# Fewer warm products, the first q in parts, a lent staging buffer and a new table of order

## The chip, the cores and the metric

The kernel runs on one core of a Trainium2 chip. The metric is device time of one launch in microseconds. Three runs of the kernel before gave 1077.51, 1078.24 and 1081.42 us; the median is 1078.24 us.

The core's engines run their own queues of instructions and wait for one another by semaphores. PE multiplies matrices (it also transposes, as a product with an identity), DVE and ACT work on rows of elements, POOL does the same more slowly, and SP issues DMAs. All data are float32.

## The reference

Attention in which only scores within `tau` of the row's largest count, then two feed-forward layers:

```python
scores = scale * q @ k.T                                  # q, k, v: 4 x 8 x 576 x 64
thresh = max(scores, axis=-1) - tau
scores = where(scores >= thresh, scores, -1e9)
attn = exp(scores - max(scores)); attn /= sum(attn) + 1e-9
x = (attn @ v) -> [2304, 512]                             # heads side by side
x = (s * relu(x @ w_in) ** 2 + b) @ w_out                 # 512 -> 2048 -> 512
h = x @ w2_in; y = (relu(h) + alpha * min(h, 0)) @ w2_out # 512 -> 2048 -> 512
```

The weights arrive as 64-bit words and are turned into float32 on the chip.

## The kernel before, in words

Three stages overlap. Attention handles 16 pairs of heads; a pair has nine score tiles of 128 rows by 576 columns. For each, PE makes the scores (line 1394), DVE takes the row maximum (1404), POOL a threshold from it (1406), ACT the exponential (1408), and DVE masks and sums (1410). The tile `e` that comes out is transposed on PE (`flip`, lines 917 to 921: all transposes of a group in the fast type in line 919, the last of a group in plain float32 in line 921, unless PE goes straight on to another group of transposes, when `plan.joined` puts that one in the fast type too), copied by ACT (1522) and multiplied by `v` (1534). The first four pairs, 36 score tiles, work in plain float32, with two buffers `sc` for the scores; the other twelve split each operand into a high and a low part and use three products.

The first feed-forward layer is cut into units of 256 hidden columns. Ten of its hidden tiles (`NA`) are prepared early, during attention: each half unit is loaded by SP into one of two staging buffers `stg` (1007, 1012), and joined to float32 in one of two buffers `n32` by DVE and ACT: line 1022 or 1024 (ACT or DVE, whichever the plan chooses), then 1028 and 1030 on DVE, the sign by 1060 on ACT and 1062 on POOL, the high part by 1066 on ACT, the low part by 1067 on POOL or DVE. The product tiles stand in `wa`. Blocks of tokens are multiplied in lines 1136 to 1138, three products for one.

The second layer, after attention, uses a scheme of seven products for eight (`seven`).

The order is not the code's. `Plan.add` records tasks, each with an engine (or several), a duration, buffers that it needs, and a rank. `Plan.run` lays them out: whenever an engine is free it takes the ready task of the lowest rank whose buffers are free. `MOVES` adds a number to the rank of task n. Buffers are slots with a count. The result is a fixed order per engine; every engine then works in that order on the chip and waits where data are late. SP waits likewise, in order, so one waiting load holds back all loads behind it.

Warm products (`warm`, line 1492) multiply the identity with itself into a spare bank: 12 at the start (`FILL`), 7 behind transposes of the first pair (`FILLS`), 3 behind each of the first two scores (`FILL1`) and 2 behind each of the other 34 of the first four pairs (`FILL2`), 93 in all. A warm product is two records in the trace.

For the first pair, SP loads k (1268) and q in one DMA each, and ACT issues the two tails (1284). PE transposes the four blocks of q; then DVE scales the copy for head 0 and ACT that for head 1 (1328, 1330).

## Time and profile before

| what | value |
|---|---|
| median of three runs | 1078.24 us |
| the profiled execution | 1078.0 us, of which 1076.0 us from the first instruction to the last |
| PE busy | 1056.9 us (98%) |
| DVE busy | 876.9 us (81%) |
| ACT busy | 695.0 us (65%) |
| POOL busy | 357.1 us (33%) |
| DMA engines, mean rate | 159 GB/s |

The busy time of an engine is the union of its instructions, so a stretch with overlapping products counts once. The shares are means over stages with different limits; the stage tables among the rows below cut them apart. The 2.0 us around the span are the launch.

### The profile page before, as it was taken

The page shows a single profiled execution, that of the slowest core. Times are in us where ns is not written, and L with a number is a line of the kernel's source. Part 1 is how long each engine was busy: PE and PEld are TensorE (multiplying, and loading weights), DVE is VectorE, ACT ScalarE, POOL GpSimd, SP SyncE. Part 2 cuts the span into 40 slices and gives each one's busy share as a digit, 9 for nine tenths or more (in the row PEclk, how much of TensorE's full clock was granted, in tenths as well). Part 3 has the DMA queues.
Part 4 walks back from the last instruction along what each step waited for, and adds up shares of the span by engine and source line. Part 5 has one row for each costly group of instructions (what it writes and reads, how often), then busy time and mean ns, then how long its engine had stood idle before and what let it go on. Part 6 is the DMA issues. An engine that isn't in the chain of part 4 may idle for free.

```text
span 1076.0 us, 21525 instructions
## 1 busy us (share of the span) xinstructions
PE 1056.9 (98%) x7210; PEld 1008.9 (94%) x7210; DVE 876.9 (81%) x1989; ACT 695.0 (65%) x1636; POOL 357.1 (33%) x494
## 2 busy tenths in 40 slices
PE   8899999999999999999999999999999999999998
PEld 7677899999989899989999999999999999999998
DVE  5989888888898888847967686588988999898882
ACT  5888878878887788744442355465756776565550
POOL 2666746744764466420000021120111344112110
PEclk9999999999999999999999999999999999999999
DMA  7754375566365644425476767249664664554531
GB/s 183 190 163 141 97 177 131 149 165 153 98 156 139 150 106 111 122 75 189 139 244 201 259 211 230 79 132 291 223 228 158 196 206 140 150 145 141 146 99 40
DMA packets 182127, 170.90 MB, mean 159 GB/s; under 512 B 56065, under 2 KB 160513, under 8 KB 182017
## 3 DMA queue, kind: packets, MB, share of 16 engines
q1 hardware_dynamic: 179248, 167.50, 54.5%
q10 hardware_dynamic: 2768, 2.03, 0.7%
q8 instruction: 56, 0.92, 0.4%
q14 instruction: 55, 0.44, 0.1%
HBM read 98.97 MB, written 49.28 MB: 138 GB/s over the span
## 4 chain that ended last, share of the span: by engine, by line
PE 86%; DVE 6%; ACT 3%; DMA 3%; issue 2%; SPq 0%; POOL 0%; DVEq 0%; ACTq 0%; POOLq 0%
PE bank L1136 14%; PE bank L1137 13%; PE bank L1138 13%; PE bank_b L1137 8%; PE bank_b L1138 8%; PE bank_b L1136 8%; PE sc L1394 7%; PE bank L1554 5%; PE bank L919 4%; PE bank L921 3%; PE bank L1492 1%; PE bank L1534 1%; DVE e L1410 1%; DVE wb L1114 1%; DMA stg<-in_moe_w_in_dram 1%
## 5 line engine op out<-in xcount | busy, mean ns | idle before, releaser
L1410 DVE SCALAR_TENSOR_TENSOR e<-sc,mx,e 128x576 f32<-128x576 f32 x144 | 116.2, 811 | 12.9 <-ACT e L1408 9.0
L1404 DVE TENSOR_REDUCE mx<-sc 128x1 f32<-128x576 f32 x144 | 107.6, 751 | 22.4 <-PE sc L1394 21.6
L1408 ACT ACTIVATE e<-sc,mx 128x576 f32<-128x576 f32 x144 | 106.6, 742 | 12.9 <-DVE mx L1404 12.4
L1136 PE MATMUL bank<-xt,wa 128*128 128x480 f32 (+3 forms) x235 | 87.0, 370 | 1.2 <-ACT rest L1676 0.8
L1406 POOL TENSOR_SCALAR mx<-mx,tau_s 128x1 f32<-128x1 f32 x144 | 51.2, 357 | 87.5 <-DVE mx L1404 80.3
L1137 PE MATMUL bank<-xt,wa 128*128 128x480 f32 (+3 forms) x235 | 79.1, 337 | 0.0
L1138 PE MATMUL bank<-xt,wa 128*128 128x480 f32 (+3 forms) x235 | 79.1, 336 | 0.0
L921 PE MATMUL bank<-eyes_r,e 128*128 128x128 f32 (+1 forms) x238 | 68.9, 291 | 0.5 <-DVE e L1410 0.5
L1554 PE MATMUL bank<-gl,vt 128*128 128x256 f32 (+1 forms) x192 | 63.6, 332 | 0.0
L1136 PE MATMUL bank<-gt,wa 128*128 128x384 f32 (+3 forms) x173 | 62.2, 360 | 0.6 <-ACT gw L1868 0.3
L1137 PE MATMUL bank<-gt,wa 128*128 128x384 f32 (+3 forms) x173 | 59.7, 345 | 0.0
L1138 PE MATMUL bank<-gt,wa 128*128 128x384 f32 (+3 forms) x173 | 59.7, 345 | 0.0
L1554 PE MATMUL bank<-gh,vt 128*128 128x256 f32 (+1 forms) x192 | 57.7, 302 | 0.0
L1592 DVE TENSOR_TENSOR gl<-bank,gh 128x256 fp32r<-128x256 f32 (+1 forms) x96 | 43.4, 452 | 10.9 <-ACT gh L1590 9.1
L1394 PE MATMUL sc<-k,q 128*128 128x288 f32 x232 | 49.0, 337 | 3.3 <-DMA q<-hq 1.5
L1101 POOL TENSOR_TENSOR sm<-stg 128x256 f32<-128x256 f32 x8 | 6.6, 835 | 135.3 <-DMA stg<-wfi 125.3
L1602 POOL TENSOR_TENSOR gr<-gf,gh 64x256 fp32r<-64x256 f32 (+1 forms) x48 | 38.9, 811 | 35.1 <-DVE gl L1600 28.3
L1136 PEld LDWEIGHTS bank<-xt,wa 128*128 128x128 f32 x235 | 45.1, 192 | 3.8 <-ACT rest L1676 1.2
L1590 ACT ACTIVATE gh<-bank 128x256 fp32r<-128x256 f32 (+1 forms) x96 | 39.4, 411 | 12.7 <-PE bank L921 5.5
L1138 PEld LDWEIGHTS bank<-xt,wa 128*128 128x128 f32 x235 | 44.1, 188 | 2.4
L1030 DVE SCALAR_TENSOR_TENSOR n<-stg,n 128x512 int32<-128x512 int32 x64 | 45.5, 710 | 0.8
L1137 PEld LDWEIGHTS bank<-xt,wa 128*128 128x128 f32 x235 | 44.5, 189 | 0.7
(686 smaller groups left out, 4190.5 us busy)
## 6 DMA issues: line engine op xcount, KB each, us to landing
stg<-in_moe_w_in_dram SPq DMA_DIRECT2D x32, 512.0 KB, 4.2
stg<-in_moe_w_out_dram SPq DMA_DIRECT2D x32, 512.0 KB, 4.0
gf<-gw SPq DMA_DIRECT2D x41, 192.0 KB, 3.2
q<-hq SPq DMA_DIRECT2D x24, 256.0 KB, 4.7
qo<-hq SPq DMA_DIRECT2D x24, 256.0 KB, 4.6
gw<-gf SPq DMA_DIRECT2D x47, 128.0 KB, 2.9
xt<-xs SPq DMA_DIRECT2D x14, 384.0 KB, 4.6
yf<-yb SPq DMA_DIRECT2D x24, 192.0 KB, 2.6
```

The source lines that it names most:

```text
L921: nc.tensor.transpose(to, part(x), one)
L1030: add("DVE", dve(DM), lambda: nc.vector.scalar_tensor_tensor(ni(), word(0), 29, ni(), op0=ALU.logical_shift_right, op1=ALU.bitwise_or), (n ...
L1136: nc.tensor.matmul(o, lhsT=wl, rhs=mh, start=first, stop=False, skip_group_check=on_top)
L1137: nc.tensor.matmul(o, lhsT=wh, rhs=ml, start=False, stop=False, skip_group_check=on_top)
L1138: nc.tensor.matmul(o, lhsT=wh, rhs=mh, start=False, stop=last, skip_group_check=on_top)
L1394: nc.tensor.matmul(sp.t[:, x, :HS], lhsT=o[0][:, c], rhs=o[1][:, x * HS:(x + 1) * HS], start=n == 0, stop=n == len(passes) - 1)
L1404: add("DVE", dve(S), lambda sp=sp, mx=mx: nc.vector.tensor_reduce(mx.t[:, 0:1], sp.t[:, :, :HS], op=ALU.max, axis=AX.XY, negate=True), (sp ...
L1406: t2 = add("POOL", 0.26, lambda mx=mx: nc.gpsimd.tensor_scalar(mx.t[:, 1:2], mx.t[:, 0:1], -1.0, tau_s, op0=ALU.mult, op1=ALU.subtract), ( ...
L1408: add("ACT", act(S, 1), lambda sp=sp, mx=mx, e=e: nc.scalar.activation(halves(e.t), sp.t[:, :, :HS], AF.Exp, bias=mx.t[:, 0:1]), (sp, mx), ...
L1410: add("DVE", dve(S) + 0.065, lambda sp=sp, mx=mx, e=e, col=col, sums=sums: nc.vector.scalar_tensor_tensor(halves(e.t), sp.t[:, :, :HS], mx ...
L1554: nc.tensor.matmul(o.t[:, :n], lhsT=w.rearrange("p a b -> p (a b)"), rhs=m.t[:, :n], start=c == first and x == 0, stop=c == last and x == ...
L1592: add("DVE", dve(n), lambda hi=hi, lo=lo, gt=gt: nc.vector.tensor_tensor(lo.t[:, :n], gt.t[:, :n], f32(hi.t[:, :n]), op=ALU.subtract), (gt ...
```

## The change

The counts of warm products become 8, 3 and 0: 34 scores lose two each and the start four, so 21 of 93 stay. The first pair's k and q come in halves by head, q also in halves by block (four DMAs of 64 KB, one of them issued by ACT), and q's two halves are transposed and scaled apart, into different banks. Five of the twenty half units (`LENT`) are staged in memory of the tenth weight tile (`stgl`, `nl`), which joins the pool of weight tiles when they are done. The plan's own figures change (when engines begin, transposes, loads), transposes of a group now come after the copies of the group before (`prior`), and `MOVES` is a new table.

```diff
-FILL, FILL1, FILL2 = 12, 3, 2
+FILL, FILL1, FILL2 = 8, 3, 0
...
+LENT = (2, 5, 8, 11, 14)
 MOVES = {
-    1: -31.56, 2: -31.95, 3: -36.63, 4: 3.891, 5: -62.75, 6: -17.94, 7: -36.26, 8: -4.312, 9: -16.56, 10: 63.66, 11: 15.14, 12: -1098, 13: -771,
...
+    0: 30.7, 1: 30.86, 2: -2.206, 3: -2.144, 4: -22.55, 5: -12.64, 6: -14.51, 7: -54.53, 8: -677, 9: -975, 10: -768.2, 11: 17.64, 12: -521.8,
...
-    JOIN = 0.05
+    BEGIN = {"PE": 1.6, "SP": 0.7, "ACT": 1.1, "DVE": 5.0, "POOL": 4.8}
+    JOIN = 0.04
...
     def turned(k):
-        return 0.112 + 0.061 * (k - 1)
+        return 0.112 if k == 1 else 0.173 + 0.085 * (k - 2)
...
-    w_s = Cuts(tiles(wp, NA, "wa", [P, 2, 4 * G1], F32R), p_s, lambda t: pieces(t.rearrange("p a n -> p (a n)")))
+    def at(name, n, dt, o):
+        return nc.alloc_sbuf_tensor_at(name, [P, n], dt, offset=o).ap()
+
+    end[0] -= 32 * G1
+    wa = [*tiles(wp, NA - 1, "wa", [P, 2, 4 * G1], F32R), at("wl", 8 * G1, F32R, end[0]).rearrange("p (a n) -> p a n", a=2)]
+    w_s = Cuts(wa[:-1], p_s, lambda t: pieces(t.rearrange("p a n -> p (a n)")))
+    lent_s = Slots([at("stgl", 2 * DM, F32, end[0])]), Slots([at("nl", DM, F32, end[0] + 8 * DM)])
+    lent = []
...
-            raw, n32, b = Buf(stg_s), Buf(n32_s), self.buf
             inner = kind.endswith("i")
+            loan = early and (f if inner else NA + f) in LENT
+            (raw, n32), b = [Buf(x) for x in (lent_s if loan else (stg_s, n32_s))], self.buf
...
+            if loan:
+                lent.append(plan.tasks[-1])
...
+            def tail_in(t, nm, src, r):
+                tl = src[b, h0:h0 + 2, NQ * P:S, :].rearrange("h p d -> p h d")
+                if p == 0 and nm == "q":
+                    add("ACT", 0.7, lambda: nc.scalar.dma_start(t.t[r, NQ], tl), (), (t,), (), -LATER, 0.5, load=carried(32, 256, 1.3))
+                else:
+                    hwdge(lambda: nc.sync.dma_start(by_head(t)[r, :, NQ] if nm == "v" else t.t[r, NQ], tl), (), (t,), base - 12 * STEP, 32, (), 256, 0.5, 0.65, 1.3)
+
...
+                for cs in {"k": (slice(0, NQ),), "q": (slice(0, 2), slice(2, NQ))}[nm] if p == 0 else (slice(0, NQ),):
+                    kb, came[nm, cs.start] = 64 * (cs.stop - cs.start), []
+                    for h in (slice(0, 1), slice(1, 2)) if p == 0 else (slice(0, 2),):
+                        def load(e, t=t, src=src, cs=cs, h=h):
+                            e.dma_start(t.t[:, cs, h], src[b, h0:h0 + 2, 0:NQ * P, :].rearrange("h (p c) d -> p c h d", c=NQ)[:, cs, h])
+
+                        if p == 0 and nm == "q" and cs.start == 0 and h.start == 0:
+                            x = add("ACT", 0.6, lambda load=load: load(nc.scalar), (), (t,), (), -LATER, 0.5, load=carried(kb / 2, 256, 1.3))
+                        elif p == 0:
+                            x = hwdge(lambda load=load: load(nc.sync), (), (t,), base - 12 * STEP, kb / 2, (), 256, 0.5, 0.5, 1.3)
...
+            qa = Buf(t=q32[p]) if p == 0 else qs[0]
...
+                for cs in ((0, 1), (2, 3), (NQ,)) if p == 0 and nm == "q" else (tuple(range(NQ)), (NQ,)):
+                    tail, hl = cs == (NQ,), qa if nm == "q" and cs == (0, 1) else of
+                    n, c0 = TL if tail else len(cs) * P, cs[0] * P
                     c = slice(c0, c0 + n)
                     s0 = TL if tail and nm == "q" else 0
...
+                        if p == 0 and not tail:
+                            add("PE", turned(len(cs)), transpose, (), (t, tr, hl), came[nm, cs[0]], rank=ready, turn=True)
+                        else:
+                            add("PE", turned(len(cs)), transpose, (t,), (tr, hl), rank=ready, turn=True)
+                        for _ in range(FILLS[nm, tail] if p == 0 and cs[0] in (0, NQ) else 0):
                             warm(-LATER, plan.tasks[-1:])
...
-                        for h in range(2):
-                            c0 = 2 * NQ * P + h * TL if tail else h * NQ * P
+                        for h in (1, 0) if p == 0 else range(2):
+                            c0 = 2 * NQ * P + h * TL if tail else h * NQ * P + cs[0] * P
...
-                        of, passes = (qs[0], ks[0]), [(q32[p], k32[p])]
+                        of, passes = (qa if ii < 2 else qs[0], ks[0]), [(q32[p], k32[p])]
...
                 add("PE", turned(2 + gi), lambda gt=gt, keys=keys, rows=rows: turned_e(gt, es, whole, h, gi, keys, rows),
-                    [es[i] for i in whole] + ([es[NQ]] if gi else []), (gt,), rank=rank, turn=True)
-                add("ACT", act(n), lambda f=f, gt=gt, rows=rows: nc.scalar.activation(
-                    f.t[:rows, :n], gt.t[:rows, :n], AF.Copy), (gt,), (f,), rank=rank)
+                    [es[i] for i in whole] + ([es[NQ]] if gi else []), (gt,), after=prior[0], rank=rank, turn=True)
+                copies.append(add("ACT", act(n), lambda f=f, gt=gt, rows=rows: nc.scalar.activation(
+                    f.t[:rows, :n], gt.t[:rows, :n], AF.Copy), (gt,), (f,), rank=rank))
                 held[h, gi, c] = f
+            prior[0] = copies
...
-            warm(-LATER)
+            warm(-LATER, us=2 * pe(P, 2))
...
+        add("POOL", 0.01, lambda: w_s.add(wa[-1:]), after=lent, rank=-2.0)
```

Other hunks change `far` and `pace` of loads in the plan (what it reckons that a load takes), nothing in the instructions.

The start of PE's order before, from the eleventh warm product to the first pair's q (`nat0` holds k, `nat1` q, `bank` the places of results; `waits` names semaphores, DMAHW those of loads):

```order
L1492 MATMUL bank_116<-eyes_r 128x128
L919 MATMUL bank_117<-eyes_r,nat0r 128x128 [waits DMAHW3_49,DMAHW2_49,DMAHW1_49]
L919 MATMUL bank_117<-eyes_r,nat0r 128x128 x2
L921 MATMUL bank_117<-eyes_r,nat_141 128x128
L1492 MATMUL bank_115<-eyes_r 128x128
L921 MATMUL bank_118<-eyes_r,nat_141 128x128
L1492 MATMUL bank_116<-eyes_r 128x128
L1492 MATMUL bank_115<-eyes_r 128x128
L1492 MATMUL bank_116<-eyes_r 128x128
L919 MATMUL bank_117<-eyes_r,nat1r 128x128 [waits DMAHW4_49,Activation_49]
L919 MATMUL bank_117<-eyes_r,nat1r 128x128 x2
L921 MATMUL bank_117<-eyes_r,nat_143 128x128
```

and now:

```order
L1519 MATMUL bank_119<-eyes_r 128x128
L920 MATMUL bank_117<-eyes_r,nat0r 128x128 [waits DMAHW4_49,DMAHW5_49,DMAHW3_49,DMAHW1_49]
L920 MATMUL bank_117<-eyes_r,nat0r 128x128 x2
L922 MATMUL bank_117<-eyes_r,nat_143 128x128
L1519 MATMUL bank_118<-eyes_r 128x128
L920 MATMUL bank_120<-eyes_r,nat0r 128x128
L920 MATMUL bank_119<-eyes_r,nat1r 128x128 [waits DMAHW6_49,DMAHW7_49,DMAHW2_49,DMAHW0_49]
L922 MATMUL bank_119<-eyes_r,nat_145 128x128
L1519 MATMUL bank_118<-eyes_r 128x128
L920 MATMUL bank_117<-eyes_r,nat1r 128x128 [waits Activation_49]
L922 MATMUL bank_117<-eyes_r,nat_145 128x128
L1519 MATMUL bank_118<-eyes_r 128x128
```

Six warm products stand ahead of k's transposes in place of eleven, one in place of three between k and q, and q's first two blocks wait for all four of q's loads.

DVE's order around the third half unit of weights before (`n` the joined numbers, `stg` the staged words, `mx` maxima, `e` exponentials):

```order
L1446 TENSOR_SCALAR rc_177<-sums_175 128x2x2
L1028 TENSOR_SCALAR n_101<-n_101 128x512
L1447 RECIPROCAL rc_177<-rc_177 128x2x2
L1404 TENSOR_REDUCE mx_172<-sc_119 128x1
L1030 SCALAR_TENSOR_TENSOR n_101<-stg_99,n_101 128x512
L1024 TENSOR_SCALAR n_102<-stg_100 128x512
L1410 SCALAR_TENSOR_TENSOR e_157,sums_174<-sc_120,mx_171,e_157 128x576
L1410 SCALAR_TENSOR_TENSOR e_159,sums_174<-sc_119,mx_172,e_159 128x576
```

and now, around the same half:

```order
L1033 TENSOR_SCALAR nl<-nl 128x512
L1474 RECIPROCAL rc_178<-rc_178 128x2x2
L1437 SCALAR_TENSOR_TENSOR e_159,sums_176<-sc_122,mx_173,e_159 128x576
L1431 TENSOR_REDUCE mx_174<-sc_121 128x1
L1355 TENSOR_SCALAR gw_108<-bank_120,by_half 128x512
L1035 SCALAR_TENSOR_TENSOR nl<-stgl,nl 128x512
L1437 SCALAR_TENSOR_TENSOR e_153,sums_176<-sc_121,mx_174,e_153 128x576
L1431 TENSOR_REDUCE mx_175<-sc_122 128x1
L1033 TENSOR_SCALAR n_103<-n_103 128x512
L1035 SCALAR_TENSOR_TENSOR n_103<-stg_101,n_103 128x512
L1437 SCALAR_TENSOR_TENSOR e_155,sums_176<-sc_122,mx_175,e_155 128x576
```

The half is staged in `stgl`, and DVE has no line 1024 (now 1029) for it: that step stands on ACT. Up to the fortieth maximum DVE has 4 of these steps where it had 8, 4 of the low parts (1067, now 1073) where it had 6, 4 squarings (1172, now 1180) where it had 2, and 4 splits (1178, now 1186) where it had 5.

SP's order of the first loads of weights before:

```order
L1007 DMA stg0_99<-in_moe_w_in_dram 128x4x256
L1286 DMA nat2_145<-in_q_dram 64x2x64
L1286 DMA nat2_145<-in_k_dram 64x2x64
L1268 DMA nat2_145<-in_k_dram 128x8x64
L1007 DMA stg1_100<-in_moe_w_in_dram 128x4x256
L1268 DMA nat0_141<-in_q_dram 128x8x64
L1286 DMA nat1_143<-in_k_dram 64x2x64
L1286 DMA nat1_143<-in_q_dram 64x2x64
L1268 DMA nat1_143<-in_k_dram 128x8x64
L1007 DMA stg0_99<-in_moe_w_in_dram 128x4x256
```

and now:

```order
L1012 DMA stg0_101<-in_moe_w_in_dram 128x4x256
L1275 DMA nat1_145<-in_k_dram 64x2x64
L1275 DMA nat1_145<-in_q_dram 64x2x64
L1288 DMA nat1_145<-in_k_dram 128x8x64
L1012 DMA stg1_102<-in_moe_w_in_dram 128x4x256
L1012 DMA stgl_99<-in_moe_w_in_dram 128x4x256
L1288 DMA nat0_143<-in_q_dram 128x8x64
L1275 DMA nat2_147<-in_k_dram 64x2x64
L1275 DMA nat2_147<-in_q_dram 64x2x64
L1288 DMA nat2_147<-in_k_dram 128x8x64
L1012 DMA stg0_101<-in_moe_w_in_dram 128x4x256
```

Three loads of weights can be under way where two could.

## Rows read from the trace of the kernel before

**Rows 1.** The page, its first line: the span of the profiled execution.
```profile
span 1076.0 us, 21525 instructions
```
**Rows 2.** Busy time by stretch: PE, PEld, DVE, ACT, POOL (x instructions), clock, DMA share, GB/s.
```profile
20.00:140.00 120.00, 114.26 (x843) 91.67 (x842) 106.58 (x230) 98.92 (x230) 78.03 (x93) 1.00 0.56 156
140.00:450.00 310.00, 305.36 (x2222) 286.01 (x2221) 267.23 (x631) 249.00 (x576) 175.12 (x263) 1.00 0.57 138
450.00:1050.00 600.00, 598.78 (x3869) 594.88 (x3868) 488.29 (x1093) 336.15 (x809) 96.60 (x109) 1.00 0.56 175
1050.00:1076.00 26.00, 21.48 (x180) 21.27 (x178) 5.55 (x15) 2.36 (x8) 1.53 (x3) 0.99 0.15 40
```
**Rows 3.** The same view of the warm products alone (line 1492): PE, PEld, clock, DMA.
```profile
20.00:140.00 120.00, 22.79 (x128) 18.89 (x128) 1.00 0.56 156
140.00:1076.00 936.00, 0.00 (x0) 0.00 (x0) 1.00 0.55 159
```
**Rows 4.** The chain of waits from 20 to 140 us, shares of the stretch by line.
```profile
by line: PE sc L1394 17.0%; PE bank L1534 10.5%; issue 8.0%; DVE e L1410 6.8%; PE bank L919 6.2%; PE bank L1492 5.4%; DMA stg<-in_moe_w_in_dram 4.6%; DVE n L1028 3.9%; ACT wa L1060 3.5%; PE bank L1136 3.2%; ACT e L1408 3.1%; PE bank L1137 2
```
**Rows 5.** Groups of DVE, 20 to 140 us: count, busy us, mean ns, idle before, releaser.
```profile
L1404 DVE TENSOR_REDUCE mx<-sc 128x1 f32<-128x576 f32 x38 | 28.4, 751 | 8.1 <-PE sc L1394 8.0
...
L1024 DVE TENSOR_SCALAR n<-stg 128x512 f32<-128x512 f32 x8 | 5.7, 708 | 1.0 <-DMA stg<-in_moe_w_in_dram 1.0
L1067 DVE TENSOR_TENSOR wa<-n,wa 128x512 fp32r<-128x512 f32 x6 | 4.8, 800 | 0.0
L1469 DVE TENSOR_TENSOR z<-z,bank 128x256 f32<-128x256 f32 x8 | 3.3, 415 | 0.0
...
L1328 DVE TENSOR_SCALAR gw<-bank,by_half 128x512 f32<-128x512 f32 x2 | 1.4, 746 | 0.0
```
**Rows 6.** Groups of ACT, 20 to 140 us, the same columns.
```profile
L1522 ACT ACTIVATE ge<-bank 128x320 f32<-128x320 f32 (+3 forms) x40 | 15.1, 409 | 0.9 <-PE bank L919 0.4 <-PE bank L921 0.2
...
L1022 ACT ACTIVATE n<-stg 128x512 f32<-128x512 f32 x12 | 8.1, 681 | 1.5 <-DMA stg<-in_moe_w_in_dram 1.5
...
L1330 ACT ACTIVATE q<-bank,by_half 128x512 f32<-128x512 f32 x1 | 0.7, 689 | 0.0
```
**Rows 7.** DVE in order of time near 38 us: start, us, instruction, idle before.
```profile
36.68 1.45 DVE L1030 SCALAR_TENSOR_TENSOR n<-stg,n 128x512 int32<-128x512 int32 x1
39.09 0.71 DVE L1024 TENSOR_SCALAR n<-stg 128x512 f32<-128x512 f32 x1 [0.97 <-DMA stg<-in_moe_w_in_dram]
```
**Rows 8.** What SP's queue waited for, 20 to 140 us: total us, times, longest.
```profile
SPq L1012 <- DVE n L1030: 32.7, 9, 7.3
```
**Rows 9.** The first 12 us in order of time, PE and ACT.
```profile
1.62 5.06 PE L1492 MATMUL bank<-eyes_r 128*128 128x128 f32 x22 [1.62 <-DVE eyes_r L1633]
...
7.65 0.83 PE L1492 MATMUL bank<-eyes_r 128*128 128x128 f32 x6
...
8.24 0.46 PE L919 MATMUL bank<-eyes_r,nat1r 128*128 128x128 f32 x3
...
9.72 0.69 ACT L1330 ACTIVATE gw<-bank,by_half 128x512 f32<-128x512 f32 x1 [1.13 <-DVE gw L1328]
...
10.46 1.24 PE L1394 MATMUL sc<-k,gw 128*128 128x288 f32 x4 [0.97 <-ACT gw L1330]
```
**Rows 10.** Loads of q in the first 9 us, from issue to landing.
```profile
DMA to landing us min/median/max: 2.2/4.1/4.8
```
**Rows 11.** Groups of PE over the span: transposes in two passes (921) and in one (919).
```profile
L921 PE MATMUL bank<-eyes_r,e 128*128 128x128 f32 x228 | 66.2, 291 | 0.5 <-DVE e L1410 0.5
...
L919 PE MATMUL bank<-eyes_r,e3r 128*128 128x128 f32 x103 | 23.9, 236 | 0.3 <-DVE e L1410 0.3
```
**Rows 12.** Two stretches of 10 us, columns as in rows 2.
```profile
40.00:50.00 10.00, 7.99 (x52) 6.04 (x48) 9.52 (x22) 7.46 (x20) 5.36 (x7) 1.00 0.80 202
150.00:160.00 10.00, 8.55 (x79) 8.37 (x78) 7.70 (x21) 6.14 (x15) 3.47 (x6) 1.00 0.78 182
```
**Rows 13.** What PE waited for, 140 to 450 us: total us, times, longest.
```profile
PE sc L1394 <- DMA q<-hq: 1.5, 1, 1.5
```

More of the change, by code (lines that the diff above doesn't have):

```diff
@@ L776, in run @@
         now = 0.0
+        for e in engines:
+            busy[e] = True
+            at(self.BEGIN[e], "free", e)
         while left:
@@ L993, in tile_kernel, with carried, hwdge @@
     moe_s = Slots(banks[3:], {"h": 1})
-    def carried(kb, part):
-        return 1.4 * kb * 1024 / part * (0.0083 + 0.0369e-3 * part) / 16
-    def hwdge(fn, reads=(), writes=(), rank=None, kb=192, after=(), part=1536, far=0.0, us=0.5):
-        return add("SP", us, fn, reads, writes, after, rank, tail=far, load=carried(kb, part))
+    def carried(kb, part, pace=1.4):
+        return pace * kb * 1024 / part * (0.0083 + 0.0369e-3 * part) / 16
+    def hwdge(fn, reads=(), writes=(), rank=None, kb=192, after=(), part=1536, far=0.1, us=0.5, pace=1.0):
+        return add("SP", us, fn, reads, writes, after, rank, tail=far, load=carried(kb, part, pace))
     def numbers(src, inner, f, raw, n32, rank, after, also=(), signs=True):
@@ L1024, in mult @@
                 on(e).tensor_scalar(n32.t, f32(word(1)), REBIAS, None, op0=ALU.mult)
-        hwdge(load, (), (raw, *also), rank, 512, after, 1024 if inner else 4096, 0.4)
+        hwdge(load, (), (raw, *also), rank, 512, after, 1024 if inner else 4096, 0.4, pace=1.4)
         add([("DVE", 0.34, rank), ("ACT", act(DM, 0, True) + 0.04, rank)], 0, mult, (raw,), (n32,), port=True)
@@ L1129, in weights @@
             raw.t.rearrange("p (h n) -> p h n", h=2), wf[kind].rearrange("(h u p) n -> u p h n", h=2, p=P)[u]),
-            [wf_d[kind][u], wf_d[kind][u + NF // 2]], (raw,), rank, 512, after, 2048, 0.3)
+            [wf_d[kind][u], wf_d[kind][u + NF // 2]], (raw,), rank, 512, after, 2048, 0.9, pace=1.2)
         q = {f"{i + 1}{j + 1}": (raw, lambda o=(2 * i + j) * G1: raw.t[:, o:o + G1]) for i in range(2) for j in range(2)}
@@ L1147, in load_x @@
             t = hwdge(lambda x=x, c=c: nc.sync.dma_start(
-                f32(x.t[:, :, :n]), src[:, c * P:(c + 1) * P, c0:c0 + n].rearrange("a p t -> p a t")), bufs[c], (x,), rank, n, chain[0], 4 * n, 0.6)
+                f32(x.t[:, :, :n]), src[:, c * P:(c + 1) * P, c0:c0 + n].rearrange("a p t -> p a t")), bufs[c], (x,), rank, n, chain[0], 4 * n, 0.8, pace=1.3)
             xs.append(x)
@@ L1276, in pair @@
                 t = nat["v" if nm == "v" else "k"]
[L1277 removed]
                 if nm == "v" and not whole:
                     x = src[b, h0:h0 + 2, 0:NQ * P, :].rearrange("h (p c) d -> p c h d", c=NQ)[P - TL:P, NQ - 1]
[L1281 to L1286 removed]
+                    hwdge(lambda t=t, x=x: nc.sync.dma_start(by_head(t)[0:TL, :, NQ], x), (), (t,), base - 12 * STEP, 32, (), 256, 0.5, 0.65, 1.3)
+                if p or nm != "k":
+                    tail_in(t, nm, src, slice(TL, P) if nm == "q" or nm == "v" and not whole else slice(0, TL))
             first = whole
@@ L1488, in parts, with warm @@
                     xs[i, (p % NP) * P:(p % NP + 1) * P, t0 + to.start:t0 + to.stop], x.t[:, c] if i == 0 else f32(x.t[:, c])), (x,), rows, rank, 0.5 * n, (), 4 * n)
-        def warm(rank, after=()):
+        def warm(rank, after=(), us=pe(P, 2)):
             w = Buf(one_s, "o")
-            add("PE", pe(P, 2), lambda: nc.tensor.matmul(w.t[:, :P], lhsT=ident, rhs=ident, start=True, stop=True), (), (w,), after, rank)
+            add("PE", us, lambda: nc.tensor.matmul(w.t[:, :P], lhsT=ident, rhs=ident, start=True, stop=True), (), (w,), after, rank)
         outs, prods, made = {}, [], [0]
@@ L1515, in plain_group @@
             whole = [base, base + 1] if gi == 0 else [base + 2, base + 3]
+            copies = []
             for c in range(NK):
@@ L1793, in tile_kernel @@
                 hwdge(lambda p=p, d=d, c0=c0, n=n: nc.sync.dma_start(p.t[:, :n], ya[d * P:(d + 1) * P, c0:c0 + n]),
-                      [x[d] for x in within(c0, n, blocks_a, ya_d)], (p,), SOON, after=(sw,), far=0.1)
+                      [x[d] for x in within(c0, n, blocks_a, ya_d)], (p,), SOON, after=(sw,), far=0.4, pace=1.4)
                 add("ACT", act(n, 1, True), lambda p=p, n=n, of_b=of_b: nc.scalar.activation(
@@ L1975, in store @@
                             nc.sync if e == "SP" else nc.scalar).dma_start(
-                            out[t0:t0 + (r - 1) * step + 1:step, o:o + G1], x.t[r0:r0 + r, :G1]), (x,), (), tail=0.3, load=carried(r, 1024))
+                            out[t0:t0 + (r - 1) * step + 1:step, o:o + G1], x.t[r0:r0 + r, :G1]), (x,), (), tail=0.1, load=carried(r, 1024, 2.1))
                         r0 += r
```

43 lines of the change are left out of this document (16 added, 27 removed), and 1184 rows, old and new, of the table MOVES.

## The prediction

> **What bounds the kernel now.** I read the page's first line for the span, 1076.0 us [rows 1], and then the busy time by stretch [rows 2], since the page's shares are means over stages with different limits. There the kernel falls in two. From 140 to 450 us PE is busy 305.36 of 310 us, from 450 to 1050 us 598.78 of 600: nothing but PE's own products can make these stretches shorter. In the first 140 us it is less plain. From 20 to 140 us PE is busy 114.26 of 120 us, but 22.79 us of that are warm products, and after 140 us there are none [rows 3]; about 91.5 us are work that the result needs. DVE is busy 106.58 us of the 120 and ACT 98.92. So the first stage is bound by DVE, with ACT and PE close behind, and by the rounds between them: PE makes a score, DVE takes its maximum, ACT its exponential, DVE masks it, and only two buffers hold scores. Third I read the chain of waits of this stage [rows 4]: scores lead with 17.0%, warm products stand on it with 5.4% and loads of weights into `stg` with 4.6%. The groups of DVE [rows 5] agree: ahead of its maxima DVE idles 8.1 us for scores, ahead of line 1024 it idles 1.0 us for a load.
>
> Since PE is full after 140 us and its needed work hardly changes, a microsecond won earlier arrives at the end undiminished, as long as the new order lets PE start the later work earlier. The profiled execution took 1078.0 us, its span and 2.0 around it, 0.24 below the median of 1078.24. I add the terms to 1078.0.
>
> **The start.** PE now runs warm products from 1.62 to 6.68 us (the first line there) [rows 9]: 22 records, 0.23 us each, the slow level; six later ones take 0.83 us, 0.14 each. The first score begins at 10.46 us, behind the scaling of q on ACT, 0.69 us, which itself stood 1.13 us behind DVE's scaling. What the change takes out of this path: one of the scalings is of half size. DVE's 512-wide one costs 0.746 us [rows 5]; I take 0.415 for the half, that of another 128x256 operation there, and a like saving on ACT: 0.3 us each, 0.6 together if the two stand one after the other. Two warm products fewer between k and q: four records at 0.14, 0.5 us. What it adds: q in four loads, and each half of q by block. By the order PE waits for all four with the first of them, so the halves let nothing begin earlier; a load of q takes 2.2 to 4.8 us from issue to landing [rows 10], and the last of the four is issued behind the others, so q may land up to the same or a little later. Also, six warm products stand ahead of k where eleven stood, 2.8 us at the pace seen. If PE is then still at its slow level when the scores begin, the first two of them, 1.24 us for the two halves of one [rows 9], cost 0.23/0.14 times as much, 0.8 us more each. The first two effects give -1.1; I take -0.8, with -2.2 (1.13 us of waiting gone besides) and +1.5 as bounds.
>
> **The stage of the first four pairs.** 72 warm products go, four at the start and 68 behind scores. At 0.14 to 0.18 us a record (0.83/6, 22.79/128) the 68 are 19 to 24 us of PE. Hardly any of that is on the path, if DVE sets the pace: PE stands idle where the product stood. It counts only where a warm product is directly ahead of a score that DVE waits for. DVE waits 8.0 us for scores over 38 maxima [rows 5], and a warm product of two records ahead of it is 0.28 us; I give it -0.4. The most that can come back is the chain's share, 5.4% of 120, 6.5 us [rows 4].
>
> What moves between engines weighs more. Up to the fortieth maximum DVE loses four of the steps of line 1024 (0.708 us each, -2.8), two low parts (0.800, -1.6) and two 512-wide scalings of q (0.746, -1.5), and gains one net 128x256 operation (two squarings more, one split less, 0.415, +0.4) [rows 5]: 5.5 us off 106.6. ACT takes the four steps, 0.681 each, and the two scalings, 0.689 each [rows 6]: +4.1, so 98.9 becomes 103.0. The busier of the two falls from 106.6 (DVE) to 103.0 (ACT), by 3.6 us. The copies behind ACT's steps, line 1522, 409 ns each and 40 of them [rows 6], are what is queued behind the moved steps; the transposes' buffers and so the products with `v` wait for them. That may eat a part, but ACT keeps 17 us of idle time.
>
> The third staging buffer. SP's queue waited 32.7 us in nine waits for the end of a join, the longest 7.3 [rows 8], since a load needs a free `stg`. Once that showed at DVE: its step at 39.09 us stood 0.97 us for the load, after the join that freed the buffer had ended at 38.13 [rows 7], and ACT's line 1022 idled 1.5 us for the same reason [rows 6]. With a third buffer that load stands one join further ahead. I take -1.0. The bounds are 0 and the chain's share of these loads, 4.6% of 120, 5.5 us [rows 4]; what is late next is the scores, 17.0% of the chain.
>
> The sum of this stage is -0.4 - 3.6 - 1.0 = -5.0, with 0 and -12 (6.5 + 5.5) as bounds.
>
> **Behind it.** Twelve transposes stand in two passes where they stood in one, since the new order puts them elsewhere: a record of line 921 takes 291 ns, of 919 236 [rows 11], 12 x 0.055 = +0.7 us. The rest of the table reorders some 900 us in which PE is full already. Its idle time is 4.6 us of 310 and 1.2 us of 600 [rows 2]; I count it at nothing either way and hold one wait that it may bring as a rival.
>
> Sum: -0.8 - 5.0 + 0.7 = -5.1, so 1078.0 - 5.1 = 1072.9 us.
>
> **A rule against the change.** In the rows, the clock is granted in full (1.00, the 2.4 GHz level) in every stretch, with warm products (40 to 50 us, PE busy 7.99 of 10) and without any (150 to 160 us, busy 8.55) [rows 12]. The Trainium skill, "TensorE: Matmul & The Clock Gate", section "What's actually happening", says that the slow level is the default, that sustained activity releases it and that idleness brings it back. By that rule the removal could be paid with slow products; the row at 150 to 160 us speaks against it there, but no row shows PE as idle as it may become at 40 to 50 us. By the rule the sum would be the third rival's; by the row it stays as above.
>
> **The rivals.**
>
> First, *nothing comes of it*: the rounds between score, maximum, exponential and mask are what sets the pace, not the sum of an engine's work; ACT's added steps delay the exponentials (3.1% of the chain now, DVE's masks 6.8%) as much as DVE's lost steps help, and PE idles where the warm products stood. For it: neither DVE (106.6 of 120) nor ACT (98.9) is full. Against it: DVE is busy 9.52 of 10 at 40 to 50 us [rows 12]. Time: 1078.0 + 0.7 - 0.8 = 1077.9. Also here belongs that q in parts doesn't do what it says, the start staying as it is: 1078.7.
>
> Second, *the chain gives all back*: warm products and staging waits leave it and nothing takes their place, -12 in the place of -5.0: 1065.9. For it: they stand on the chain. Against it: DVE would have to do 101 us of work in 108 us, fuller than now.
>
> Third, slower, *the clock falls*: in the stage without warm products PE drops to 1.2 GHz. Per 10 us PE's needed work is 7.99 less 1.9 (22.79/12), 6.1 us at 40 to 50 us, and 7.6 on the mean (91.5/12); at half the pace that is 12.2 to 15.2, so 2.2 to 5.2 us over, 3.7 in the middle. One such stretch costs most of the gain, the second makes the kernel slower than before (-5.1 + 7.4), the third brings -5.1 + 11.1 = +6.0: 1084.0. For it: six of the first 28 records stand at the fast pace only after 5 us of products without a gap. Against it: the clock reads 1.00 at 150 to 160 us with a busy share of 8.55.
>
> Fourth, slower as well, *the new table starves PE later*: between 140 and 450 us PE once waits 1.5 us for a load of split q now [rows 13]. Each further wait of this kind costs 1.5; four undo the gain (-5.1 + 6.0), seven make 1083.5.
>
> **How the numbers follow.** Forecast 0.56 (its own range 1068 to 1077, from half of the -3.6 not arriving and a start of +1.5, to half of what the chain can still give), first rival 0.20, second 0.11, third 0.08, fourth 0.05. A measurement of this kernel can tell about 0.5% from no change, 5.4 us: below 1072.85 is faster, above 1083.63 slower. The forecast lies on the lower bound, so about half of its 0.56 goes to each side, 0.29 and 0.27; with the second rival whole and a little of the first, faster is 0.43. The third and fourth together are slower by so much in about 0.11, the rest of them and the first rival's is the same, 0.46. The range for 8 in 10 reaches from 1066.5, which leaves the second rival's lower half out, to 1080, which takes in the first rival and the slower ones while they are mild.
>
> **What would show it.** In the profile after: the stretch from 20 us to the end of the first four pairs shorter by some 5 us, with PE's busy share down to 80% or less; DVE's busy time to that point lower by 5 us and ACT's higher by 4; SP's waits for `stg` well below 32.7 us and no idle time ahead of line 1024 (now 1029); the first score at about 9.7 us; clock 1.00 throughout. It is wrong if the scores' durations double anywhere, if PE after the first stage has more than 6 us of idle time, or if DVE's idle time grows by what its work shrinks.

## The result

The kernel after took 1068.97 us (median of four runs, 1068.82 to 1072.25), the one before 1077.92 (four runs): a ratio of 0.9917, 95% interval 0.9889 to 0.9945, 9 us less. In a later comparison on one chip it was 0.9916 (0.9904 to 0.9928). The forecast was 1072.9, its range 1066.5 to 1080: the sign and the range hold, the gain is 1.8 times the forecast, and most of its terms were far from what they turned out to be.

The profiled execution took 1068.96 us. Its span, and the stretches of [rows 2] (columns as there):

```profile
span 1067.1 us, 21196 instructions
```
```profile
20.00:140.00 120.00, 109.52 (x782) 84.95 (x782) 112.17 (x236) 106.29 (x247) 80.95 (x99) 1.00 0.60 167
140.00:450.00 310.00, 308.29 (x2228) 287.92 (x2227) 271.14 (x643) 253.50 (x588) 177.02 (x266) 1.00 0.55 137
450.00:1050.00 600.00, 597.42 (x3861) 593.60 (x3860) 485.11 (x1082) 320.68 (x780) 84.46 (x96) 1.00 0.56 174
```

With three records of warm products left PE is busy 109.52 us of these 120, not the 80% or less that I expected. That has two reasons. The prediction took the 22.79 us of [rows 3] off PE's 114.26, but they are the union of the warm products' own records, which overlap with their neighbours: with 68 of these products taken out of the same order (the first experiment below) PE is still busy 105.89 us, 8.4 less:

```profile
20.00:140.00 120.00, 105.89 (x721) 79.01 (x719) 106.33 (x232) 99.82 (x232) 78.77 (x94) 0.99 0.54 154
```

The other reason is that PE takes over products of the first layer that stood later: 185 records of lines 1144 to 1146 (before, 1136 to 1138) in the stretch where it had 150. DVE is at 112.17 and ACT at 106.29 of 120; in the kernel before both were less busy, 106.58 and 98.92 [rows 2]. The stage didn't get its time from less work of its busiest engine, but from engines that wait less. The waits of DVE say for what (us in total, times, longest), and the two groups that answer to [rows 5]:

```profile
DVE mx L1431 <- PE sc L1421: 2.2, 5, 0.8
```
```profile
L1431 DVE TENSOR_REDUCE mx<-sc 128x1 f32<-128x576 f32 x40 | 29.9, 750 | 2.6 <-PE sc L1421 2.2
...
L1029 DVE TENSOR_SCALAR n<-stg 128x512 f32<-128x512 f32 x2 | 1.9, 958 | 0.0
...
L1029 DVE TENSOR_SCALAR nl<-stgl 128x512 f32<-128x512 f32 x2 | 0.8, 416 | 0.0
```

Ahead of its maxima DVE now waits 2.2 us for scores where it waited 8.0, and the four steps of line 1029 on a staged half have no idle time ahead where the eight of line 1024 had 1.0. The chain of waits of the same stretch, for [rows 4]:

```profile
by line: PE sc L1421 10.6%; issue 8.4%; DVE e L1437 6.7%; DMA stg<-in_moe_w_in_dram 5.0%; ACT ge L1550 4.9%; PE bank L920 4.9%; ACT e L1435 4.8%; PE bank L1144 4.7%; DVE mx L1431 4.3%; ACT wa L1066 4.0%; PE bank L1145 4.0%; PE bank L1146 3.
```

Scores fell from 17.0% to 10.6%; warm products (1519) are not on it; loads into `stg` still are, with 5.0%. SP's waits for staging buffers, against 32.7 us [rows 8]:

```profile
SPq L1017 <- DVE n L1035: 24.8, 5, 14.4
SPq L1017 <- DVE nl L1035: 9.2, 2, 6.3
```

They did not shrink (24.8 + 9.2); with the waits at the other line of these loads it is 38.2 us where it was 41.8. SP still stands in line, but by its order its loads stand one join further ahead. The start, for [rows 9]:

```profile
1.62 2.93 PE L1519 MATMUL bank<-eyes_r 128*128 128x128 f32 x12 [1.62 <-DVE eyes_r L1662]
5.30 0.42 PE L920 MATMUL bank<-eyes_r,nat0r 128*128 128x128 f32 x3 [0.74 <-DMA nat<-in_k_dram]
...
7.88 1.24 PE L1421 MATMUL sc<-k,gw 128*128 128x288 f32 x4 [0.69 <-ACT gw L1357]
```

The first score begins at 7.88 us instead of 10.46. Of these 2.6 us 1.5 lie ahead of k's transposes (5.30 instead of 6.80) and 1.1 between them and the score. In a second profile of the same kernel it begins at 8.13 and runs slower (last section). Where the time came from is best seen at equal needed work: I gave each needed record of PE the mean pace of its shape after 140 us in the kernel before, and asked when so much of it was done. The kernel after is ahead by 2.6 us at 1 us of it, 5.1 at 20 us, 9.8 at 70, 11.4 at 120 and still 11.4 or more at 300, but 9.6 at 500 and 9.4 at the end. So, as an estimate: 2.6 from the start, 9 from the stage of the first four pairs and shortly behind it, and 2 given back in the later stage. The steps in between move by 1 to 2 us with the pace that is given to a record, the 9.4 does not. The second profile is ahead by 1.6 us at 1 us and by 9.1 at the end.

### The profile page after: what moved, and what is told of

Its sections match the earlier page's. It is cut to its first block, busy times and chain, and to the rows that moved or that the text cites. A ratio compares the mean times of both kernels' runs of the same rounds, so it can differ in the third digit from the quotient of the medians.

```text
span 1067.1 us, 21196 instructions
## 1 busy us (share of the span) xinstructions
PE 1043.7 (98%) x7066; PEld 991.9 (93%) x7066; DVE 882.3 (83%) x1992; ACT 691.9 (65%) x1639; POOL 348.8 (33%) x490
## 4 chain that ended last, share of the span: by engine, by line
PE 80%; DVE 8%; ACT 5%; DMA 4%; issue 2%; SPq 1%; POOL 0%; DVEq 0%; ACTq 0%
PE bank L1144 13%; PE bank L1145 13%; PE bank L1146 12%; PE bank_b L1145 8%; PE bank_b L1144 8%; PE bank_b L1146 8%; PE sc L1421 6%; PE bank L1583 5%; PE bank L920 4%; PE bank L922 3%; DVE e L1437 1%; DMA stg<-in_moe_w_in_dram 1%; DMA stg<-in_moe_w_out_dram 1%; ACT e L1435 1%; DVE mx L1431 1%
## 5 line engine op out<-in xcount | busy, mean ns | idle before, releaser
L1431 DVE TENSOR_REDUCE mx<-sc 128x1 f32<-128x576 f32 x144 | 107.4, 750 | 10.6 <-PE sc L1421 9.7
L1144 PE MATMUL bank<-xt,wa 128*128 128x480 f32 (+3 forms) x227 | 83.4, 368 | 0.6 <-ACT rest L1175 0.6
L1145 PE MATMUL bank<-xt,wa 128*128 128x480 f32 (+3 forms) x227 | 76.6, 337 | 0.0
L1146 PE MATMUL bank<-xt,wa 128*128 128x480 f32 (+3 forms) x227 | 76.4, 336 | 0.0
L1144 PE MATMUL bank<-gt,wa 128*128 128x384 f32 (+3 forms) x144 | 51.4, 357 | 1.1 <-ACT gt L1196 0.7
L1145 PE MATMUL bank<-gt,wa 128*128 128x384 f32 (+3 forms) x144 | 49.8, 346 | 1.0 <-DVE gt L1197 1.0
L1146 PE MATMUL bank<-gt,wa 128*128 128x384 f32 (+3 forms) x144 | 49.7, 345 | 0.0
L1619 ACT ACTIVATE gh<-bank 128x256 fp32r<-128x256 f32 (+1 forms) x96 | 39.4, 410 | 11.4 <-PE bank L922 6.4
L1144 PEld LDWEIGHTS bank<-xt,wa 128*128 128x128 f32 x227 | 43.8, 193 | 2.5 <-ACT rest L1175 1.4
L1616 POOL TENSOR_TENSOR gl<-gf,gh 128x256 fp32r<-128x256 f32 (+1 forms) x48 | 38.7, 806 | 21.7 <-ACT gh L1614 9.8
L1421 PE MATMUL sc<-k,q 128*128 128x288 f32 x200 | 43.7, 346 | 1.7 <-DMA qo<-hq 0.9
L1196 ACT ACTIVATE gt<-rest 128x384 fp32r<-128x384 f32 x56 | 29.3, 524 | 24.3 <-DVE rest L1194 23.7
L1146 PEld LDWEIGHTS bank<-xt,wa 128*128 128x128 f32 x227 | 42.6, 188 | 2.4
L1193 ACT ACTIVATE rest<-bank_b 128x384 f32<-128x384 f32 x29 | 14.2, 490 | 45.8 <-PE bank_b L1146 45.8
```

What stands on the lines that cost most here:

```text
L1144: nc.tensor.matmul(o, lhsT=wl, rhs=mh, start=first, stop=False, skip_group_check=on_top)
L1145: nc.tensor.matmul(o, lhsT=wh, rhs=ml, start=False, stop=False, skip_group_check=on_top)
L1146: nc.tensor.matmul(o, lhsT=wh, rhs=mh, start=False, stop=last, skip_group_check=on_top)
L1421: nc.tensor.matmul(sp.t[:, x, :HS], lhsT=o[0][:, c], rhs=o[1][:, x * HS:(x + 1) * HS], start=n == 0, stop=n == len(passes) - 1)
L1431: add("DVE", dve(S), lambda sp=sp, mx=mx: nc.vector.tensor_reduce(mx.t[:, 0:1], sp.t[:, :, :HS], op=ALU.max, axis=AX.XY, negate=True), (sp ...
```

## The experiments

Ratios are to the kernel before on the same chip; a difference of 0.001 is 1.1 us. All but the two without the lent buffer keep the order of their base on every engine, row for row, except for the instructions named.

**Warm products taken from the kernel before.** The 68 tasks behind scores stay in the plan and issue nothing:

```diff
-  add("PE", pe(P, 2), lambda: nc.tensor.matmul(w.t[:, :P], lhsT=ident, rhs=ident, start=True, stop=True), (), (w,), after, rank)
+  add("PE", pe(P, 2), lambda: nc.tensor.matmul(w.t[:, :P], lhsT=ident, rhs=ident, start=True, stop=True) if on else None, (), (w,), after, rank)
```

> The kernel before, in its own order on every engine, but the 68 warm products behind the 34 scores issue nothing. Theory A (DVE, ACT and the rounds between them set the pace of the first stage, PE merely idles where a warm product stood): -0.4 us, at most -1.5, so about 1077. Theory B (warm products stand on the chain of waits): -4 to -6.5 us, 1071.5 to 1074. Theory C (the clock needs them): granted clock falls between 20 and 140 us, +2 us or more. This is the part of the change's 9 us that fewer warm products bring by themselves.

Measured 1075.63 us, ratio 0.9996 (0.9982 to 1.0009). Theory A: nothing to speak of. But theory C was in the profile too. The stretches around it, and what DVE waited for:

```profile
48.00:51.40 3.40, 1.74 (x10) 1.29 (x12) 3.40 (x7) 3.40 (x9) 2.02 (x2) 0.98 0.35 91
51.40:54.70 3.30, 3.30 (x18) 1.80 (x20) 2.89 (x7) 1.62 (x3) 2.03 (x4) 0.51 0.99 289
```
```profile
DVE mx L1404 <- PE sc L1394: 9.2, 12, 2.4
```

PE was busy 1.74 of 3.4 us, and then the granted clock read 0.51, the 1.2 GHz level, for 3.3 us. So the run alone could not say whether nothing was to be had or the clock took it. In five of its twelve executions the mean granted clock was 0.999 or 1.000, and their median is 1074.88 us; in the other seven, at 0.997 or 0.998, it is 1076.55, and the kernel before took 1076.45 on that chip. So the lost clock likely cost something, and what it may have hidden is of the size of 1.5 us.

**Seven warm products where PE stood**, on top of the kernel above: three ahead of its fifteenth score, four behind.

```diff
+HOLES = {(14, 2): 3, (15, 2): 4}
...
+        for _ in range(HOLES.get(tuple(self.at), 0)):
+            self.fill()
```

`at` counts scores and PE's tasks behind the last; `fill` is one warm product.

> The kernel before in its own order, without its 68 warm products behind scores, but with seven others, three ahead of the fifteenth score and four behind it, where PE stood 0.85 and 1.0 us and the granted clock then read 0.50 from 51.4 to 54.7 us. Theory A (in the old order DVE, ACT and the rounds set the pace, whatever PE does): as without them, ratio 0.998 to 1.000. Theory I (taking the 68 away does gain in the old order too, and the lost clock took it back): 1.5 to 2.5 us less than without them, ratio 0.997 to 0.998.

Measured 1075.31 us, 0.9993 (0.9983 to 1.0002), and the clock in its profile is whole:

```profile
50.00:60.00 10.00, 8.14 (x57) 5.83 (x57) 9.26 (x20) 8.45 (x21) 6.32 (x8) 1.00 0.91 255
```
```profile
DVE mx L1413 <- PE sc L1403: 7.8, 13, 1.1
```

Theory A: in the old order the products cost at most 2 us (the interval's end), likely 0.7; DVE waits for scores as long as before.

**Warm products put back into the kernel after**, two behind each of the same 34 scores (behind the next where no bank was free):

```diff
                                     start=n == 0, stop=n == len(passes) - 1)
+                        if more:
+                            made[1] += 2
+                        if more and one_s.free:
+                            for _ in range(made[1]):
+                                nc.tensor.matmul(one_s.free[0][:, :P], lhsT=ident, rhs=ident, start=True, stop=True)
+                            made[1] = 0
```

> The kernel after, in its own order, with 68 warm products put back behind the same 34 scores (two behind each, or four behind the next where no bank is free). Theory A: +0.4 us, at most +1.5, about 1069.5 to 1070.5. Theory B: +4 to +6.5, 1073 to 1075.5. PE has less slack in the changed first stage than in the one before (91% busy without warm products), so it should cost no less than it did before.

Measured 1079.08 us, 1.0016 (1.0004 to 1.0028), 10.8 us more than after, beyond theory B: the whole gain is gone. DVE's wait and the chain, 20 to 140 us:

```profile
DVE mx L1437 <- PE sc L1421: 5.8, 13, 1.0
```
```profile
by line: PE sc L1421 22.9%; PE bank L1569 12.9%; PE bank L1428 9.7%; PE bank L920 7.9%; PE bank L1144 4.9%; PE bank L1145 4.4%; PE bank L1146 4.4%; PE bank L922 4.0%; issue 3.9%; DVE e L1443 3.9%; ACT ge L1556 2.7%; ACT e L1441 1.7%; DVE mx
```

Scores are back at 22.9% of the chain, the products themselves (1428) at 9.7%. Not all of the loss arises there, at least in this profile, which is of one of the two longest of twelve executions (1080.61): near 488 us PE stands 3.1 us for ACT's line 1196, and then works at the slow level:

```profile
488.00:492.00 4.00, 1.97 (x5) 1.57 (x6) 3.80 (x9) 3.05 (x7) 0.00 (x0) 0.64 0.76 273
492.00:496.00 4.00, 4.00 (x14) 4.00 (x13) 2.80 (x7) 1.18 (x3) 0.00 (x0) 0.50 0.59 168
```

Counted at equal needed work as above, some 8 us are lost ahead of that place. Half the dose (`+= 1`):

> The kernel after, in its own order, with 34 warm products put back, one behind each of 34 scores (two where the bank was not free before): half the dose of the run in which 68 cost 8 to 10 us. Theory D (in the new order the first stage has so little room on PE that each warm product's 0.22 us lands on the path): about half, +3.5 to +5, 1072.5 to 1074. Rival E (a threshold: PE had 10 of 120 us idle there, 34 products take 7.5 of them and only more than that costs): +0 to +1.5, 1069 to 1070.5.

Measured 1072.02 us, 0.9953 (0.9939 to 0.9967), 4.0 us more than after: theory D's 3.5 to 5, though it is 37% of 10.8 rather than half, and more than rival E allows. Per product that is 0.12 us here and 0.16 with 68; taking them out of the old order freed some 0.13 us of PE each (8.4 us for the 64 between 20 and 140 us) and brought next to nothing. Both runs put the products into an order that was laid out without them; an order laid out for the lent buffer with the products in it was not run.

**The four loads of q.** In the kernel after q comes in one load:

```diff
+                            if p == 0 and nm == "q":
+                                if cs.start or h.start:
+                                    return
+                                cs, h = slice(0, NQ), slice(0, 2)
```

> The kernel after, in its own order, but the first pair's q comes in one load again, issued by ACT where the first of four was, 256 KB; the other three issue nothing. As predicted (q's first blocks wait for all four loads anyway, so four bring nothing): no change, 1069 +-0.5. Rival: four loads on several queues land sooner than one, so one load delays the first score by 0.5 to 1.5 us and the end by as much, 1070 to 1070.5.

Measured 1069.87 us, 0.9941 (0.9925 to 0.9957), 2.7 us more than after by the ratios. Its start:

```profile
6.62 0.60 PE L920 MATMUL bank<-eyes_r,nat0r 128*128 128x128 f32 x3 [2.06 <-DMA nat<-in_k_dram]
```

k's transposes begin 1.3 us later than in after: k's second half, issued at 2.17 us in both, landed at 6.33 us instead of 5.17, with 256 KB of q issued ahead of it in place of 64. The rival holds: against the second profile of after, whose first scores were slow too, the first score is 1.4 us late (9.51 instead of 8.13), and the 2.7 at the end are 0.5 to 4.8 by the two intervals. But it isn't q that gains, it is k. That the size of q's load ahead of it is the cause is argued, not shown: the edit also lets SP go on sooner, so that the next pair's k (256 KB) is issued at 2.85 us instead of 4.51, right behind k's second half.

**Warm products of the start.** The kernel before without the last four of twelve:

```diff
-            warm(-LATER)
+            warm(-LATER, on=x < 8)
```

> The kernel before, in its own order, but the last four of the twelve warm products at the start issue nothing. As predicted (they cover a wait for k's and q's loads): 0 to -0.5 us. Rival, from the trace of after, in which the transposes of k begin at 5.30 us instead of 6.80: the warm products themselves held PE until 6.68 us while k lay ready, and q's load, landed by 6.4 us, is the next limit: the first score some 1.2 to 1.5 us earlier, 1076.5. If four fewer leave PE at its slow level when the scores begin, +1 us instead.

Measured 1075.53 us, 0.9993 (0.998 to 1.0005). The rival fell:

```profile
1.63 3.78 PE L1492 MATMUL bank<-eyes_r 128*128 128x128 f32 x16 [1.63 <-DVE eyes_r L1633]
6.87 0.43 PE L919 MATMUL bank<-eyes_r,nat0r 128*128 128x128 f32 x3 [1.46 <-DMA nat<-in_q_dram]
...
10.34 1.24 PE L1394 MATMUL sc<-k,gw 128*128 128x288 f32 x4 [0.97 <-ACT gw L1330]
```

PE ended them at 5.41 us and then stood 1.46 us, for q's tail (landed at 6.73 us), which lies in one tile with k's. The first score came at 10.34.

The kernel after with none of its 21:

```diff
-  lambda: nc.tensor.matmul(w.t[:, :P], lhsT=ident, rhs=ident, start=True, stop=True)
+  lambda: None
```

> The kernel after, in its own order, with none of its 21 remaining warm products. If PE's level depends on them only at the start (third rival of the prediction, confined to the start): the first scores at the slow level, +0.8 us each for two to six of them, and the first score's begin no earlier since k's load sets it: +1 to +4 us, 1070 to 1073, unless the loss is recovered later, as in the run with q in one load (3 us late at the first score, 0.9 us at the end). If they cost without bringing anything: -0.5 to 0, 1068.5 to 1069.

Measured 1072.24 us, 0.9959 (0.9946 to 0.9972), 4.6 us more. In its profile, of the shortest of five executions (1070.61), the first two scores ran at the slow level by their durations, eight records in 4.18 us instead of some 2.4. That accounts for 1.8 us; where the rest arises the profile of this one execution does not show.

```profile
8.11 4.18 PE L1421 MATMUL sc<-k,gw 128*128 128x288 f32 x8 [0.73 <-ACT gw L1357]
```

With two more (they fell behind k's transposes, not ahead of them as I had meant, since the plan had put those two tasks there), and with the three between k and the first score moved to the front:

```diff
-            warm(-LATER, us=2 * pe(P, 2))
+            warm(-LATER, us=2 * pe(P, 2), n=2 if x < 2 else 1)
```

> The kernel after, in its own order, with two more warm products at the start, eight instead of six ahead of k's transposes. In one of the two profiles of after PE ran k's and q's transposes and the first score at the slow level (the score 2.01 us instead of 1.24), in the other at the fast one. If longer activity brings PE to the fast level in each execution: 0.5 to 1 us less on the mean, ratio 0.990 to 0.991 (after: 0.9916), at the price of k's transposes 0.2 us later; if not, the same or +0.3 us.

```diff
+            warm(-LATER, us=2 * pe(P, 2), n=(0, 0, 1, 1, 2, 1, 1, 2)[x])
...
+                            warm(-LATER, plan.tasks[-1:], n=len(plan.tasks) != 29)
```

> The kernel after, in its own order, with the warm products of the start moved forward: eight instead of six ahead of k's transposes, and the three between them and the first score taken away (two products too many between k and q had cost 1.4 us at the first score and as much at the end). If what stands between k and the first score is on the path, and longer activity ahead of it keeps PE at the fast level: the first score at 7.5 to 7.9 us instead of 7.9 to 8.1 and 0.3 to 1 us less at the end, ratio 0.990 to 0.9915 (after: 0.9916). If PE stays slow at the first scores all the same, as without any warm products: +1 to +3 us, ratio 0.993 to 0.995.

Measured 1068.59 us, 0.9930 (0.9918 to 0.9942), and 1067.43 us, 0.9924 (0.991 to 0.9937). In the first the first score begins at 8.96 us, 0.8 to 1.1 us later than in the two profiles of after: what stands between k and the first score is on the path there. The 1.5 us more at the end lie within the two intervals. The second, meant as a version better than both, is not told apart from after; its first score ran at the fast level but came at 8.14 us, behind ACT's scaling:

```profile
8.14 1.24 PE L1421 MATMUL sc<-k,gw 128*128 128x288 f32 x4 [0.92 <-ACT gw L1357]
```

**The third buffer.** By the new table the plan finds no order without the buffer, so tasks are ranked by the times (`WHEN`) at which they began in the plan of after, which changes the order too:

```diff
-LENT = (2, 5, 8, 11, 14)
+LENT = ()
-        t.ways = [(e, u, (r + MOVES.get(n, 0), n)) for e, u, r in ways]
+        t.ways = [(e, u, ((WHEN[n][1] if e == WHEN[n][0] else 1e7) if n in WHEN else r, n)) for e, u, r in ways]
```

> The kernel after without the lent buffer: the five half units stage in the two common buffers, tasks are ranked by the times at which they began in the plan of after, so that the order stays as near as the smaller memory lets it (the first rows of SP agree in 97%, of PE in 86%, of DVE in 73%). Warm products as in after. If the third buffer is worth what the prediction gave it (its load waits): +1 us, 1070. If it is what lets the new order pack DVE's work (5.8 us less waiting for scores): +4 to +8, 1073 to 1077. Theory F (the removal of warm products is what counts, in any order but the old): +0 to +1.

Measured 1074.98 us, 0.9985 (0.9972 to 0.9998), 7.4 us more than after. DVE waits for scores again, and the clock fell twice, after stretches like the first of these; in all twelve executions the mean granted clock is 0.993 to 0.998, in the five of after on that chip 0.999 or 1.000:

```profile
DVE mx L1431 <- PE sc L1421: 6.9, 11, 2.0
```
```profile
56.00:59.70 3.70, 1.87 (x14) 1.21 (x12) 3.23 (x10) 3.70 (x11) 2.53 (x3) 0.97 0.68 212
59.70:66.10 6.40, 6.08 (x24) 3.52 (x26) 4.32 (x13) 4.26 (x10) 4.35 (x6) 0.50 1.02 226
76.20:79.10 2.90, 2.90 (x12) 2.31 (x13) 2.87 (x7) 1.67 (x5) 1.32 (x2) 0.56 0.15 41
```

With 12 warm products in the places where PE stood:

```diff
+HOLES = {(19, 3): 4, (19, 5): 2, (19, 7): 2, (24, 2): 1, (24, 3): 3}
```

> The kernel after without the lent buffer, in the order of the run before this one that lacked it (1.0 to 1.7% behind after; its granted clock read 0.50 from 60 to 66 and from 77 to 79 us, after stretches in which PE stood for ACT), with 12 warm products put just where PE stood idle there: behind scores 19 and 24. Theory G (the lent buffer's worth is mostly the clock: without it PE stands long enough to lose its level, and 6.4 + 2.9 us at half pace cost some 4 to 5 us): granted clock 1.00 in the first stage and 3 to 5 us less than without them, ratio 0.994 to 0.996, about 1070 to 1072. Theory H (its worth is the loads' earlier landing, and the clock only follows): within 1 us of the run without them, ratio 0.998.

Measured 1076.79 us, 1.0001 (0.9989 to 1.0012): no gain. Theory G is not borne out, though not settled either: the clock stayed whole where it had been lost (from 76 to 79 us it reads 1.00), and fell elsewhere, from 36 to 40 us and from 70 to 74. By an estimate, the 8.98 us that PE worked in the two slow stretches without the fill would be 4.5 at the fast level, so up to about that much of the 7.4 may be the clock's.

```profile
30.00:40.00 10.00, 7.65 (x45) 4.99 (x45) 9.37 (x19) 8.15 (x21) 5.36 (x8) 0.83 0.56 163
...
60.00:70.00 10.00, 8.05 (x55) 5.45 (x53) 8.86 (x24) 9.21 (x22) 7.78 (x9) 1.00 0.92 219
70.00:80.00 10.00, 9.61 (x55) 7.71 (x56) 6.82 (x17) 6.99 (x17) 5.21 (x6) 0.83 0.44 123
```

```profile
DVE mx L1440 <- PE sc L1430: 6.9, 13, 2.2
```

DVE's 6.9 us of waiting stands in both runs. The control:

> The kernel after, unchanged, as the base for the others of this call: 1069 us, ratio to before 0.990 to 0.994.

Measured 1067.88 us, 0.9916.

## Why the prediction was right in sign and short in size

- *The frame held.* PE is full after 140 us, so what the first stage wins arrives: 9.4 of 11.4 us at PE's end, 8.9 in the span.
- *The start, -0.8, was -2.6* (-2.3 in the second profile), beyond its bound of -2.2. The two effects that it counted, -1.1, have the size of what was won between k's transposes and the first score, 1.1 us. What it missed are the 1.5 us ahead of these transposes. The step that failed is "by the order PE waits for all four with the first of them, so the halves let nothing begin earlier". It looked at what PE waits for and not at when that lands: in before k landed at 4.92 us, q at 6.41 and q's tail, for which k's transposes wait too, at 6.66; in after that tail landed at 4.81, the last part of k at 5.17 and of q at 5.96, though that was issued at 4.00. With q in one load k's transposes begin at 6.62 us, nearly as late as before, and 2.7 us of the total are lost again. That q in parts might not do what it says fell with it.
- *The warm products, -0.4, were right in the old order* (-0.4 and -0.7 measured, both within noise) *and wrong in the sum.* Their 19 to 24 us of PE were some 9 by that count, since the records overlap; so the 91.5 us of needed work, the 80% and the third rival's 6.1 and 7.6 us in 10 were too low. And I added that term to the others as if each could be had alone. Taking the products away brings nothing in the old order; putting them back costs 10.8 us in the new one. The old order had no use for PE's time, the new one has no room for theirs.
- *DVE's work, -5.5 to the fortieth maximum, came out as +0.7* (its busy time from the start to the end of that maximum, 133.72 us before and 125.63 after):

```profile
0.00:133.72 133.72, 124.96 (x891) 100.42 (x892) 110.93 (x242) 103.06 (x236) 79.70 (x115) 1.00 0.57 154
0.00:125.63 125.63, 111.71 (x760) 84.50 (x761) 111.65 (x237) 105.50 (x244) 80.30 (x117) 1.00 0.60 166
```

The steps, low parts and scalings that left DVE did take some 7 us off, but other records took longer than the rows that I priced them by: the squarings 0.88 us each instead of 0.415, and the joins of line 1035 and the scalings of `e` in line 1445, the same in number, 3.0 us more in all. Why is not shown. ACT's work rose by 2.4, not 4.1. So "the busier of the two falls by 3.6", the largest term of the sum, did not happen at all. The maximum ends 8.1 us earlier because DVE stands idle 14.0 us up to it instead of 22.8; its wait for scores, which I had priced at 0.4, fell by 5.8. That the time lies in the range is thus in good part luck: gains that I had priced too low stand in the place of one that did not come.
- *The third buffer, -1.0, is likely mis-sized as well*: without it 7.4 us are gone. I priced the one wait of DVE for a load. What I take it to do is to let joins and scores be laid out so that PE is not kept from the next score; that is argued, not shown. The two kernels differ in order too (DVE's first rows agree in 73%) and in the granted clock, so buffer, order and clock are shown together, not apart.
- *Behind it, +0.7*: some 2 us were given back between 300 us of PE's needed work and its end. By the stretches above PE's idle time fell from 4.6 to 1.7 us between 140 and 450 us and rose from 1.2 to 2.6 between 450 and 1050. Its waits behind 300 us are small ones, 2.7 us in all, the largest sum 1.0 us in two for line 1197. What of it is the twelve slower transposes wasn't tried.
- *The rivals.* The first, that PE idles where the products stood, is true of the old order. The second, that the chain gives all back, came nearer than the forecast (1065.9 is 3.1 us off, 1072.9 is 3.9), and DVE is as full as its counter-argument held against it: 112.17 of 120 us, which is 101 in 108. The third, the clock, is real in kernels near this one (0.51 and 0.50 for 3 to 6 us), but in after it reads 1.00 in every 10 us from 20 to 140. The rule that I set against the change, slow after idleness (the Trainium skill, "TensorE: Matmul & The Clock Gate", section "What's actually happening"), agrees with these rows as to the direction, though PE was not wholly idle ahead of the fall (busy 1.74 of 3.4 us). The fourth, a starved PE behind 140 us, did not come: one wait of 0.9 us for split q stands where one of 1.5 stood (and seven such waits would have made 1083.4, not 1083.5).

What stays open: how much the new table would bring with the old staging, and the third buffer in the old order. Neither has a run. Open as well: what of the 7.4 us is the clock, and why the same work takes DVE longer in the new order.

## What to carry to other kernels

In this kernel filler work cost next to nothing as long as nothing waited behind it, so taking it out alone showed nothing; it paid only with an order that uses the room, and that order showed nothing with the filler put back. Price such edits in pairs (each with and without the other), not as terms of a sum. The price of filler on a pipelined engine is what the engine's busy time falls by without it (8.4 us here), not the busy time of its own records (22.8). And of the first loads of a kernel, look at when each lands and what else is in flight around the one that is waited for, not only at how many the consumer waits for.
